# A second z buffer beside the first expert weights, a main load ahead of the last z stores, and another order in the last stage

## The chip, the cores and the metric

The kernel runs on one core of a Trainium2 chip. The metric is device time in microseconds of one execution; lower is better. The kernel before took 805.2 us (median of three runs, 803.65 to 806.26). Its profiled execution took 801.52 us, of which the profile's span covers 799.5 us; times below without another name are counted from the start of that span.

## The reference, cut to what matters

```python
# long convolution over the sequence, by FFT: x (8, 5696, 128), h (5696, 128)
y = irfft(rfft(x, n=2*S, axis=1) * rfft(h, n=2*S, axis=0)[None])[:, :S, :]
# soft mixture of experts on the 45568 rows of y: phi (128, 32), w1 (8, 128, 1024), w2 (8, 1024, 128)
logits = y @ phi
d = softmax(logits over all rows)        # column softmax: it needs every row
slot_in = d.T @ y                        # 32 slots, 4 for each of 8 experts
slot_out[e] = relu(slot_in[e] @ w1[e]) @ w2[e]
c = softmax(logits over the 32 slots)    # row softmax
out = c @ slot_out
```

The output can only be made when the last row of y has been through the column softmax and the experts.

## The kernel before, in words

**The convolution** is a transform in two factors, 90 and 64, written as small matmuls. Batch by batch (h first, then the eight of x) it goes through these stages: `low` and `high` (first transform, L240; result to DRAM in `fl` and `fh`), `loadf` (L274, reads it back in another order as tile `gt`), `forward` (L287 on TensorE, the product with the filter's spectrum on VectorE, L306 and L313), `backward` (L328, evicted by ScalarE into `zst`, L333). What `backward` leaves is stored to DRAM in two parts: the **main** rows in `zm`, which the first eight of a batch's twelve steps fill, and the **rest** rows in `zr`, which the steps 9 to 12 fill. A store isn't issued at once: it is put on a list, and the word `flush` issues the list.

**The pairs.** The second half works on 32 pairs, numbered T, four for each batch; 28 to 31 are those of the last batch. For a pair, on one line each:

- `loadz` (`load_main`, L377) brings 1 MB of main rows into the next buffer of the list `zring`; `loadr` (`load_rest`, L392) brings the rest rows (0.5 MB for the first and second pair of a batch, 1 MB for the third and fourth pair together); `load` does both.
- `product` multiplies them on TensorE (L419 on the main rows, L424 on the rest rows, into the same four banks) and folds the first result on ScalarE and VectorE (L427, L428, L411, L412).
- `sums` adds the rest: L411 and L412 into `op` and `om`, then two additions of `op` on GpSimd (L437) and two of `om` (L437: on GpSimd too, but on VectorE in the last stage).
- `turn` (L447, L449) transposes, `logits` (L456, L461) multiplies by phi, `maximum` (L465, L470, L473) keeps the running column maximum `low` and its step `df`, `exponent` (L487, L491, L496, L500) makes the transposed logits `L` and the column exponentials `dt`, `tokens` (L505, L508) turns `dt` into `d`, `dispatch` (L546, L551) adds to the slot sums `acc`.
- The row softmax: `shift` (maximum L514 on VectorE, subtraction L515 on GpSimd), `exp` (L521 on ScalarE), `rowsum` (L526 to L528 on VectorE), `scale` (L533 on GpSimd), `weights` (L570, transposes the combination weights).

**Where the combination weights go.** The output stage reads them from one tile `cT`. It has room only when the convolution's tiles are gone, so the pairs 0 to 24 write their weights to DRAM (L580, L581). In the last stage `fetch` loads them back in chunks of four pairs (L586, 720 KB, into a ring `cl` of two buffers), and `place2` copies two of the four quarters of a chunk into `cT` on GpSimd (L591, two copies). When the fourth quarter of a chunk is copied, `place` itself calls `fetch_c` for a further chunk. That load needs the buffer of the chunk just copied, so it waits on GpSimd. It is issued on SyncE's queue (SP), as all loads and stores of this stage are, and that queue is in order.

**The order** is written out by hand: a long string of words, each calling one function, fixes the order of issue on every engine at once. Each engine works in order and waits by semaphores.

**Memory.** Tiles come from pools that are opened and closed by hand. `lead` (tiles of the first transform) is closed after `forward` 96, and `w1s`, the first expert weights, takes its place. `front` (filter spectrum, `gt`, `zst`) is closed at the end of the convolution; the pool `last` takes its place. Before the change the list `zring` holds one buffer, `zc`, until then. `zd`, in `last`, is the second, so that no load can go to it before everything that used the memory under it is done.

**The end.** After pair 31: `join` (L598 to L610) brings the four partial maxima together, `inputs` (L784 to L797) makes the experts' inputs `siz`, `hidden` (L807, L812, L814), `flip` (L820, L822) and `second` (L831) are the experts, `outputs` (L840 to L844) makes `so4`. Then the output stage multiplies `cT` by `so4` (L889) and writes 23 MB.

Of the kernel before, what the change touches and what calls it, by code (L numbers as in the profile page):

```python
# [12 lines left out]
F32 = mybir.dt.float32  # L13
# [62 lines left out]
def kernel(  # L76
# [25 lines left out]
    P = 128  # L102
    B, S, D = x.shape
# [6 lines left out]
    CH = 4  # L110
# [245 lines left out]
    zring = [ypool.tile([P, 2, CH, 2, D], F32, name="zc")]  # L356
# [292 lines left out]
    def run(words, batch=0):  # L649
        for word in words.split():  # L650
            name, n = re.fullmatch(r"([a-z]+)(\d*)", word).groups()
            stages[name](*[int(n) + batch * strides.get(name, NQ)] if n else [])
# [26 lines left out]
    for g in range(4):  # L679
# [36 lines left out]
    lead.close()  # L716
    wts = inner.enter_context(tc.tile_pool(name="wts", bufs=1, side="right"))
    w1s = wts.tile([P, E, F], F32, name="w1s")
    run(
# [12 lines left out]
    front.close()  # L732
    rings.append(mid.enter_context(tc.tile_pool(name="ps2", bufs=4, space=PSUM)))
    last = work.enter_context(tc.tile_pool(name="last", bufs=1))
    tail["last"] = last
    zring.insert(0, last.tile([P, 2, CH, 2, D], F32, name="zd"))
    rests.insert(0, last.tile([P, 2, 2, CH, D], F32, name="zy"))
    tail["cT"] = last.tile([P, B, R1, 2 * NJ], F32, name="cT")
    second = inner.enter_context(tc.tile_pool(name="second", bufs=1, side="right"))
# [97 lines left out]
    def join_experts():  # L837
# [8 lines left out]
                  zero=zero_slots, inputs=expert_in, hidden=layer_1, flip=turn_h, second=layer_2,  # L846
                  outputs=join_experts)
    run(
# [11 lines left out]
    assert not (Ls or ys or ds or prods or gs or zs or rest or xs or folded or kept or landed or held)  # L860


# [79 lines left out]
```

## Time and profile before

| what | value |
|---|---|
| median of three runs | 805.2 us (803.65 to 806.26) |
| profiled execution | 801.52 us, span 799.5 us |
| busy share of the span | PE 89%, DVE 79%, ACT 54%, POOL 51% |
| DMA over the span | 353 GB/s |
| last pair's product (L419 on pair 31) starts | 703.15 us |
| `so4` done (VectorE, L844) | 735.35 us |
| output stage | 735.5 us to the end, 398 to 406 GB/s from 750 to 790 us |

PE is TensorE, DVE VectorE, ACT ScalarE, POOL GpSimd, SP SyncE's queue, which here only issues DMAs. In a timeline a row is: start, duration of the group (both us), engine, line, operation, output<-input, shapes, count, and in square brackets how long the engine had been idle before it and what ended the idle time. A row of SP is the issue of a DMA, not its transfer.

### The profile page before, as it was taken

The numbers are of one execution on the slowest core, as the hardware profiler recorded it, in microseconds if no ns is written. First come the engines' busy times: TensorE is split into PE (matmuls) and PEld (weight loads), VectorE is DVE, ScalarE is ACT, GpSimd is POOL, SyncE is SP. The second block draws the span as 40 slices with busy tenths as digits, with TensorE's granted clock in tenths as the row PEclk, the third lists the DMA queues.
The fourth block names the chain that finished last, engine by engine and source line by source line (L and its number), as shares of the span: only waits on it lengthen the run. The fifth ranks groups of instructions, "written<-read, shape, count | busy, mean of one in ns | idle before, by whom it ended". The sixth has DMA issues, their size and how long they took to land.

```text
span 799.5 us, 21830 instructions
## 1 busy us (share of the span) xinstructions
PE 709.9 (89%) x8884; PEld 361.7 (45%) x8884; DVE 629.6 (79%) x895; ACT 428.6 (54%) x868; POOL 410.4 (51%) x368
## 2 busy tenths in 40 slices
PE   6858689869999999999999999999998877888892
PEld 2212233324555444444544455555444444456782
DVE  1039877747999999898999899999998997895542
ACT  2423244426666666666666666666564544674442
POOL 6744242415655666666566666655533453687000
PEclk9989999989999999999999999999999999999765
DMA  8989999999999999999999999999999898873998
GB/s 291 362 301 367 367 380 385 339 360 377 388 345 382 382 396 339 387 388 383 352 396 392 374 365 400 387 359 373 358 333 307 301 376 279 323 280 125 379 401 354
DMA packets 164778, 282.49 MB, mean 353 GB/s; under 512 B 9448, under 2 KB 128872, under 8 KB 158440
## 3 DMA queue, kind: packets, MB, share of 16 engines
q1 hardware_dynamic: 163960, 280.80, 97.1%
q8 instruction: 70, 1.15, 0.5%
q10 hardware_dynamic: 720, 0.31, 0.1%
q14 instruction: 28, 0.23, 0.1%
HBM read 148.54 MB, written 132.53 MB: 352 GB/s over the span
## 4 chain that ended last, share of the span: by engine, by line
PE 62%; DMA 17%; DVE 9%; ACT 5%; issue 2%; SPq 2%; POOL 2%; DVEq 0%; ACTq 0%; POOLq 0%
PE bank L240 21%; PE bt L287 10%; PE bz L328 8%; PE bank L419 6%; DMA out_dram<-o 5%; PE bank L424 4%; PE bank L447 3%; DMA fl<-fst 3%; DMA zx<-zr 3%; PE bank L456 2%; PE bank L546 2%; DVE yf L313 2%; DVE yf L306 2%; DVE bt L306 2%; DMA gt<-fl 2%
## 5 line engine op out<-in xcount | busy, mean ns | idle before, releaser
L216 POOL TENSOR_TENSOR x<-xc 128x512 f32<-128x512 f32 x144 | 179.0, 1275 | 82.9 <-PE bank L240 65.4
L240 PE MATMUL bank<-x,s 128*32 128x512 f32 x1728 | 205.8, 608 | 12.5 <-POOL x L216 7.3
L242 ACT ACTIVATE fst<-bank 128x512 f32<-128x512 f32 x216 | 125.2, 595 | 92.4 <-PE bank L240 76.6
L287 PE MATMUL bt<-gt,wt 64*64 64x256 f32 x1620 | 117.9, 400 | 27.2 <-DMA gt<-fl 10.7
L333 ACT ACTIVATE zst<-bz 128x1024 f32<-128x1024 f32 x96 | 93.0, 969 | 79.4 <-PE bz L328 75.9
L437 POOL TENSOR_TENSOR y<-y,op 128x512 f32<-128x512 f32 x64 | 78.2, 1222 | 107.2 <-DVE op L411 104.7
L306 DVE TENSOR_TENSOR yf<-bt,Hi 128x1024 f32<-128x1024 f32 x96 | 112.5, 1172 | 21.4 <-PE bt L287 21.4
L313 DVE TENSOR_TENSOR yf<-bt,yf 128x512 f32<-128x512 f32 x192 | 119.4, 663 | 3.3
L306 DVE TENSOR_TENSOR bt<-bt,Hr 128x1024 f32<-128x1024 f32 x96 | 113.0, 1177 | 0.0
L240 PEld LDWEIGHTS bank<-x,s 128*32 128x32 f32 x1728 | 53.8, 111 | 127.8 <-issue 88.7
L328 PE MATMUL bz<-yf,vt 64*64 64x256 f32 x1440 | 100.9, 389 | 5.3 <-DVE yf L313 4.8
L287 PEld LDWEIGHTS bt<-gt,wt 64*64 64x64 f32 x1620 | 54.7, 135 | 89.5 <-issue 46.2
L533 POOL TENSOR_TENSOR L<-L,rs 128x512 f32<-128x512 f32 x32 | 34.0, 1063 | 109.2 <-DVE rs L528 90.0
L328 PEld LDWEIGHTS bz<-yf,vt 64*64 64x64 f32 x1440 | 55.1, 136 | 40.9 <-DVE yf L313 12.1
L437 POOL TENSOR_TENSOR y<-y,om 128x512 f32<-128x512 f32 x54 | 64.1, 1188 | 2.1
L427 ACT ACTIVATE y<-bank 128x512 f32<-128x512 f32 x32 | 19.1, 597 | 81.4 <-PE bank L424 81.3
L419 PE MATMUL bank<-zc,im 64*64 64x512 f32 x480 | 60.2, 599 | 0.0
L447 PE MATMUL bank<-ident,y 109*128 109x109 f32 x512 | 58.7, 261 | 1.2 <-ACT yt L449 0.7
L447 PEld LDWEIGHTS bank<-ident,y 109*128 109x128 f32 x512 | 49.7, 141 | 10.1 <-issue 6.8
L449 ACT ACTIVATE yt<-bank 128x360 f32<-128x360 f32 x128 | 52.2, 476 | 1.3 <-PE bank L447 1.2
L306 DVE TENSOR_TENSOR yf<-bt,turn 128x1024 f32<-128x1024 f32 (+1 forms) x12 | 14.0, 1171 | 47.7 <-PE bt L287 47.7
L889 PE MATMUL op<-so,cT 32*128 32x128 f32 x704 | 44.4, 367 | 5.7 <-ACT o L897 5.2
(99 smaller groups left out, 852.9 us busy)
## 6 DMA issues: line engine op xcount, KB each, us to landing
fl<-fst SPq DMA_DIRECT2D x72, 512.0 KB, 7.6
gt<-fl SPq DMA_DIRECT2D x72, 512.0 KB, 6.0
zm<-zst SPq DMA_DIRECT2D x64, 512.0 KB, 9.3
zc<-zm SPq DMA_DIRECT2D x30, 1024.0 KB, 8.8
fh<-fst SPq DMA_DIRECT2D x36, 512.0 KB, 8.3
xc<-in_x_dram SPq DMA_DIRECT2D x32, 512.0 KB, 6.4
out_dram<-o SPq DMA_DIRECT2D x16, 1024.0 KB, 10.1
gt<-fh SPq DMA_DIRECT2D x27, 512.0 KB, 7.5
```

The source lines that it names most:

```text
L216: nc.gpsimd.tensor_tensor(out=y_[:, o, :, :], in0=near, in1=far, op=AL.subtract if o else AL.add)
L240: nc.tensor.matmul(p[i * m:(i + 1) * m, :], s1[:, q + o, cols], columns(c_, o), start=True, stop=True)
L242: nc.scalar.activation(st[:, :, q, :], p[:, :].rearrange("p (n d) -> p n d", d=D), AF.Copy)
L287: nc.tensor.matmul(bt[q * HP:(q + 1) * HP, a, o, :], wt[r, 2 * i + q, :], t_[r, 2 * o + q, :, :].rearrange("p c d -> p (c d)"), start=True ...
L306: nc.vector.tensor_tensor(out=p_, in0=pv, in1=h_, op=AL.mult)
L313: nc.vector.tensor_tensor(out=y_[r, 0:k, c, :], in0=pv[:, :, c, :], in1=y_[r, 0:k, c, :], op=op_)
L328: nc.tensor.matmul(bz[a * HP:(a + 1) * HP, q, o, :], vt[r, i, a, :], y_[r, a * m + o, :, :].rearrange("p c d -> p (c d)"), start=True, sto ...
L333: nc.scalar.activation(zst[:, e_, 0:m, 0:n, :].rearrange("p o q x -> p q o x"), bz[:, 0:n, 0:m, :], AF.Copy)
L419: nc.tensor.matmul(ps[o, c][h_ * HP:(h_ + 1) * HP, :], im[r, c, :], zt[r, h_, :, c, :], start=True, stop=False)
L437: eng.tensor_tensor(out=part_, in0=part(v, 0), in1=o_[:, :, :], op=sign)
L447: nc.tensor.transpose(p[:, i * TR:(i + 1) * TR], ys[T][0:TR, k * CH + i, 0:D], ident[0:TR, 0:TR])
L449: nc.scalar.activation(yt[:, k * CH:(k + 1) * CH, :, :], of_tokens(p), AF.Copy)
```

## The change

The buffer `zd` is allocated right after `w1s`, in the memory that `lead` leaves; from there on the main loads alternate between `zd` and `zc`, pair 25 being the first into `zd`. `loadz28` moves out of the last stage to a place between the `flush` that issues the stores of `backward` 105 and that of `backward` 107. In the last stage the words stand in another order.

```diff
     w1s = wts.tile([P, E, F], F32, name="w1s")
+    zring.insert(0, wts.tile([P, 2, CH, 2, D], F32, name="zd"))
...
-        "maximum25 fetchv5 product26 sums26 backward103 flush loadz27 exponent25 flush "
-        "forward105 backward104 tokens25 shift25 exp25 flush forward106 backward105 dispatch25 "
-        "forward107 backward106 flush rowsum25 flush scale25 turn26 backward107 weights24 "
-        "logits26 flush maximum26 ")
+        "maximum25 fetchv5 product26 sums26 backward103 flush loadz27 exponent25 flush forward105 "
+        "backward104 tokens25 shift25 exp25 flush forward106 backward105 dispatch25 forward107 "
+        "backward106 flush loadz28 rowsum25 flush scale25 turn26 backward107 weights24 logits26 "
+        "flush maximum26 ")
...
-    zring.insert(0, last.tile([P, 2, CH, 2, D], F32, name="zd"))
...
-        "loadz28 loadr28 product27 exponent26 clear shift26 sums27 flush tokens26 spread "
-        "weights25 load29 fetchv6 fetchv7 exp26 fetch fetch dispatch26 flush rowsum26 product28 "
-        "turn27 scale26 sums28 logits27 weights26 maximum27 exponent27 shift27 loadz30 zero "
-        "loadr30 product29 tokens27 exp27 place2 turn28 rowsum27 dispatch27 sums29 loadz31 flush "
-        "scale27 logits28 product30 maximum28 exponent28 place2 turn29 tokens28 shift28 exp28 "
-        "sums30 rowsum28 weights27 logits29 fetchw0 fetchw2 scale28 maximum29 place2 dispatch28 "
-        "exponent29 shift29 product31 turn30 place2 sums31 tokens29 logits30 exp29 weights28 "
-        "place2 rowsum29 fetchw4 dispatch29 scale29 maximum30 turn31 exponent30 logits31 fetchw6 "
-        "flush shift30 weights29 tokens30 exp30 place4 maximum31 rowsum30 exponent31 dispatch30 "
-        "tokens31 scale30 join dispatch31 shift31 weights30 exp31 inputs rowsum31 scale31 place32 "
-        "hidden0 hidden1 flip0 flip1 second0 second1 weights31 outputs ")
+        "loadr28 product27 exponent26 clear shift26 sums27 flush tokens26 spread weights25 fetch "
+        "load29 fetch fetchv6 fetchv7 exp26 dispatch26 flush rowsum26 product28 turn27 scale26 "
+        "place2 sums28 logits27 weights26 maximum27 exponent27 place2 shift27 loadz30 zero "
+        "loadr30 product29 tokens27 exp27 place2 turn28 rowsum27 dispatch27 sums29 loadz31 flush "
+        "scale27 place2 logits28 product30 maximum28 exponent28 turn29 tokens28 shift28 exp28 "
+        "sums30 place2 rowsum28 weights27 logits29 fetchw0 fetchw2 scale28 maximum29 place2 "
+        "dispatch28 exponent29 shift29 product31 turn30 sums31 tokens29 logits30 exp29 weights28 "
+        "rowsum29 fetchw4 dispatch29 scale29 maximum30 turn31 exponent30 logits31 fetchw6 flush "
+        "maximum31 shift30 weights29 tokens30 exponent31 exp30 dispatch30 tokens31 rowsum30 join "
+        "dispatch31 scale30 inputs place2 shift31 exp31 rowsum31 place2 scale31 place32 hidden0 "
+        "weights30 hidden1 flip0 flip1 second0 second1 weights31 outputs ")
```

No instruction is added or taken away; the number of copies into `cT` stays 28.

## The prediction

> **What bounds the kernel now.** I read the chain that ended last, from its end. From 740 us it is the output stores: 398 to 406 GB/s, so this stage starts when `so4` is done and takes what it takes; time won or lost before `so4` (735.35 us) reaches the end one for one. Going back, the last stage hangs on TensorE and VectorE in turn, and its entry is in TensorE's timeline:
>
> ```profile
> 674.12 1.09 PE L546 MATMUL bank<-y,d 128*32 128x129 f32 x32 [0.31 <-ACT d L508]
> 675.77 1.95 PE L419 MATMUL bank<-zd,im 64*64 64x512 f32 x16 [0.56 <-DMA zd<-zm]
> 679.18 1.12 PE L424 MATMUL bank<-zy,ir 26*64 26x512 f32 x16 [1.46 <-DMA zy<-zr]
> ...
> 692.38 1.95 PE L419 MATMUL bank<-zd,im 64*64 64x512 f32 x16
> 694.25 1.11 PE L424 MATMUL bank<-zx,ir 26*64 26x512 f32 x16
> ```
>
> Pair 28 waits for both its loads, pair 30 for neither. Next SP's timeline, since these loads stand in that queue:
>
> ```profile
> 667.68 2.60 SPq L224 DMA_DIRECT2D zr<-zst  x4
> 670.40 0.55 SPq L377 DMA_DIRECT2D zd<-zm  x1
> 672.23 0.32 SPq L392 DMA_DIRECT2D zy<-zr  x1
> ...
> 677.77 0.32 SPq L377 DMA_DIRECT2D zd<-zm  x1
> 679.15 0.32 SPq L392 DMA_DIRECT2D zx<-zr  x1
> 687.02 0.32 SPq L377 DMA_DIRECT2D zc<-zm  x1
> 698.21 0.32 SPq L586 DMA_DIRECT2D cl<-c_t  x1
> ```
>
> The third chunk of weights (698.21) waits for GpSimd's copies of the first (696.48 to 698.18), behind all main loads: harmless. DMA moves 420 to 426 GB/s from 685 to 692.5 us and is all but idle (46 and 58 GB/s) from 695 to 700. Then GpSimd's and VectorE's timelines:
>
> ```profile
> 679.18 1.05 POOL L533 TENSOR_TENSOR L<-L,rs 128x512 f32<-128x512 f32 x1 [0.49 <-DVE rs L528]
> 683.07 2.77 POOL L437 TENSOR_TENSOR y<-y,op 128x512 f32<-128x512 f32 x2 [2.85 <-DVE op L411]
> ...
> 696.48 1.70 POOL L591 COPY cT<-cl 128x352 f32<-128x352 f32 x2
> ```
> ```profile
> 714.39 0.74 DVE L470 SCALAR_TENSOR_TENSOR low<-mx,low 128x1 f32<-128x1 f32 x1
> 715.16 0.97 DVE L473 TENSOR_TENSOR df<-low 128x1 f32<-128x1 f32 x1
> 716.06 0.67 DVE L514 TENSOR_REDUCE rm<-L 128x16 f32<-128x512 f32 x1
> 716.82 0.53 DVE L465 TENSOR_REDUCE mx<-lt 128x1 f32<-128x360 f32 x1
> 717.38 0.49 DVE L470 SCALAR_TENSOR_TENSOR low<-mx,low 128x1 f32<-128x1 f32 x1
> 717.91 0.80 DVE L473 TENSOR_TENSOR df<-low 128x1 f32<-128x1 f32 x1
> ```
>
> VectorE has no gap from 696.05 to 720 us. L470 and L473 take 0.16 us when GpSimd is idle (668.77, 668.96) and 0.49 to 0.97 here, beside its copies and softmax steps.
>
> **Pair 28: 2.05 us earlier.** Main load 28 moves from 670.40 to behind the stores of step 9, about 664.9. DMA moves only 184 to 232 GB/s from 662.5 to 672.5, so 1 MB fits. What it can delay are the stores of step 11 (issued from 667.68, landed 672.02): at most its own 2.5 us (1 MB at 420 GB/s), at least nothing; I take 0.3, as it starts nearly 3 us ahead of them. The rest load, issued at 672.5, then has nothing in front. Idle-queue rows give 2.5 us to landing for 180 KB and 4.2 for 720 KB; in between, 512 KB takes 3.5: landed at 676. TensorE ends L546 at 675.2, runs L419 (1.9) and starts L424 at 677.1, not 679.18. If the stores lose the full 2.5, this gain is gone.
>
> The second buffer also lets load 25 start about 2 us earlier (at 617.92 it waited for pair 24's L419). Pairs 25 to 27 wait for no load, and step 106, which waits 2.11 us for `gt` at 657.66, sits 40 us later: nothing, at most 0.3 us either way.
>
> **Pair 30: a new wait.** The new order copies two quarters before `sums28` and two after it. The second two free the first chunk's buffer, so the fetch of the third chunk is now issued there, on SP **ahead of** loads 30 (main and rest) and 31. It waits for GpSimd: L533 ends 680.23, two copies (1.76) 682.0, L437 (2.77) 684.75, two copies (1.70) **686.45**. Queued behind it: the three loads, issued 677.77 to 687.02 before. By 686.45 the earlier bytes (4.6 MB from 672.5, at the 256 to 423 GB/s of before) are just through. So 720 KB land 4.2 us on, 690.65; main load 30 2.5 later, 693.15; rest load 30 **695.65**. L424 of pair 30 starts there instead of 694.25: **+1.4**. TensorE would have reached it at 693.0 (pair 29's work gains 1.3, as ScalarE waits for `low` of pair 27, now beside copies), so bounds are -1.25 and +2.4 (1 us more of latency).
>
> The Trainium skill, "DMA: Bandwidth & Descriptors", section "Anatomy of one DMA — SWDGE (gpsimd) path", fits 2.0 us plus bytes at 436 GB/s for one DMA on another path. As an estimate by that, the three loads would be in at 694.95 and the sum 0.7 smaller.
>
> **Pair 31: copies away.** VectorE carries the delay to 716. GpSimd's additions for pair 31 no longer start 0.8 late behind a copy, but then they lead VectorE's by 0.7, as in pairs 28 and 29, where VectorE's two took 2.64 and 2.70 instead of 2.29: +0.35. Then L527 falls from 0.44 to 0.17, L470 of pair 30 to about 0.5 (`scale29` still beside it), its L473 and both of pair 31 to 0.16, and L514 (0.67) steps behind them: 0.27 + 0.24 + 0.81 + 0.33 + 0.64 + 0.67 = 2.96. But ScalarE's order (the L496 of pair 30, four `cT` evictions, `d`, L491) takes over as the limit; following it row by row, `dt` of pair 31 ends 5.95 us after VectorE's additions, not 7.30: **-1.35**, with ends 0 and -2.96.
>
> The Trainium skill, "SBUF — State Buffer", section "Who interferes with whom", says a VectorE instruction with two SBUF inputs blocks against a GpSimd one that reads SBUF. It speaks against a larger gain: the copies moved to 680 to 709 block L470 and L473 of pairs 27 and 29 in turn; 0.79 and 0.80 at 704.93 fit.
>
> **`join`.** `exp30` (L521, 717.89 before) now follows `dt` of pair 31 on ScalarE, and `rowsum30` (1.1 us), which needs it, stands ahead of L600 on VectorE. Before, `dt` ended at 719.68 and `acc` of pair 31 began at 722.68, 3.0 later. Now: L521 0.9 after `dt`, three sums 1.15, L600 and L602 0.6, L604 and L546 1.5: 4.2. **+1.2**, between 0 (if L521 slips in early) and 1.6.
>
> **Experts.** `weights30` (L570) moves from the shadow of `acc` between `hidden0` and `hidden1`: **+0.55**; `shift31` moves behind `siz`, so L521 holds ScalarE's first eviction, about hidden by that. The 12 copies left (14 before) end near 738.5, ahead of the batch that needs them.
>
> **Sum:** 1.4 + 0.35 - 1.35 + 1.2 + 0.55 = **+2.15 us**. The profiled execution (801.52) would become 803.7; the median of the runs is 3.7 above it, and 805.2 + 2.15 = **807.4**.
>
> **Rivals.**
> - *The lead reaches the end (faster).* If the fetch is over before pair 30 needs its loads (-1.25 in place of +1.4), and `exp30` costs nothing in `join`: -1.25 + 0.35 - 1.35 + 0 + 0.55 = -1.7; with VectorE rather than ScalarE the limit behind pair 31 (-2.96) -3.3, 801.9. For it: VectorE is packed and copies demonstrably stretch it. Against it: the queue's order is fixed, and so is ScalarE's. Decides: rest load 30 landed before 693.
> - *No stall, but `join` late:* -1.25 + 0.35 - 1.35 + 1.2 + 0.55 = -0.5, 804.7.
> - *The fetch waits longer (slower).* Additions of 3.29 us (710.13) and slower copies put it at 687.5, and loads interleave, as the 6.9 us of pair 28's rest load suggest: L424 at 697.5, +3.25; sum +4.0, 809.2. Decides: fetch after 687.
> - *The load ahead does nothing:* the stores lose all it gains. Pair 30 decides anyway: still about +2.
>
> **The numbers.** Forecast with the last rival (+0.8 to +3.2) 0.52; slower rival 0.20; no stall 0.15; faster rival 0.13. Within 0.3% (2.4 us, about what runs of this kernel can tell apart) lie two thirds of the forecast's 0.52 and most of the no-stall case: 0.46. Slower: 0.20 and a third of the forecast, 0.39. Faster: 0.15 with the edge of the no-stall case. The range reaches into both outer rivals: 802.6 to 810.0.
>
> **What would show it.** Right: L424 of pair 28 at about 677, SP's third fetch at about 686.5 with loads 30 behind it, L424 of pair 30 waiting for DMA to about 695.6, L526 of pair 30 just ahead of L600, L473 of pairs 30 and 31 at 0.16. Wrong: no DMA wait at pair 30, or `acc` of pair 31 within 3 us of `dt`.

## The result, and the profile after

The changed kernel took 813.0 us (median of six runs, 811.2 to 814.1), the kernel before beside it 805.6: a ratio of 1.0106, 95% interval 1.0083 to 1.0128, so about 8.5 us slower by that ratio (the two medians lie 7.5 apart). The forecast was 807.4 with a range up to 810.0: the sign of the forecast was right, the size was not, and the range missed.

The profiled execution took 814.07 us (span 812.3). Of the 12.8 us between the two spans 0.9 lie ahead of pair 27; so I count from the start of pair 27's L419, at 667.45 before and 668.31 after. This pair of traces overstates the difference: the changed kernel's profiled execution is the slowest of its six, while that of the kernel before (801.52) lies below all its six.

TensorE's timeline of the changed kernel (the rows of pairs 28 and 30):

```profile
676.81 2.77 PE L419 MATMUL bank<-zc,im 64*64 64x512 f32 x16
681.75 1.93 PE L424 MATMUL bank<-zy,ir 26*64 26x512 f32 x16 [2.17 <-DMA zy<-zr]
...
699.26 3.48 PE L419 MATMUL bank<-zc,im 64*64 64x512 f32 x16 [3.04 <-DMA zc<-zm]
```

Two things differ from the forecast. Pair 28, which was to reach L424 at 677, reaches it at 681.75, and still waits for its rest load. Pair 30 waits, as forecast, but for the *main* load and 3.04 us, and then the sixteen matmuls of L419 take 3.48 us instead of 1.95. That row, and the 2.77 and 1.93 us of pair 28, lie where TensorE's granted clock (1.00 is full speed) is about half: 0.52 from 675 to 677.5 and from 700 to 702.5, 0.50 from 682.5 to 685. SP's timeline shows what stood in the queue:

```profile
666.25 1.04 SPq L377 DMA_DIRECT2D zc<-zm  x1
...
668.54 3.72 SPq L224 DMA_DIRECT2D zr<-zst  x4
677.38 0.33 SPq L392 DMA_DIRECT2D zy<-zr  x1
...
691.31 0.33 SPq L586 DMA_DIRECT2D cl<-c_t  x1
691.73 0.38 SPq L377 DMA_DIRECT2D zc<-zm  x1
```

The main load of pair 28 stands ahead of the last stores; the rest load, which must wait until they have landed, is issued 8.8 us after the first of them, where it was 4.6 before. The third fetch is issued at 691.31 (forecast 686.45), with pair 30's loads right behind it, as forecast. Why it is so late is in GpSimd's timeline:

```profile
677.24 0.13 POOL L768 MEMSET y<- 128x16 f32 x1 [8.98 <-DMA zr<-zst]
...
683.73 1.74 POOL L591 COPY cT<-cl 128x360 f32<-128x360 f32 x2 [0.63 <-DMA cl<-c_t]
...
689.12 2.15 POOL L591 COPY cT<-cl 128x352 f32<-128x352 f32 x2
```

L768, the memset of a `y` buffer, waits for the last stores from `zst` (before, at 672.38, it waited for ScalarE), and the softmax of pair 26 and the copies that free the fetch's buffer follow in GpSimd's order. The copies also wait 0.63 us for the first chunk itself.

The end, TensorE's timeline:

```profile
726.97 0.27 PE L598 MATMUL bank<-ident,low 128*1 128x128 f32 x1
729.44 0.35 PE L604 MATMUL bank<-one,lr 1*128 1x1 f32 x2 [2.20 <-DVE lr L602]
729.72 1.95 PE L546 MATMUL bank<-y,d 128*32 128x129 f32 x32
...
734.23 3.64 PE L807 MATMUL bank<-w1s,siz 128*32 128x512 f32 x16 [0.28 <-DVE siz L797]
```

and the same stretch in windows of 2.5 us. The columns are the window, its length, busy time and count of PE, PEld, DVE, ACT and POOL, then TensorE's granted clock, DMA share (the mean busy share of the 16 DMA engines) and GB/s. First after:

```profile
727.50:730.00 2.50, 0.56 (x10) 0.55 (x14) 1.64 (x6) 0.66 (x2) 0.97 (x1) 0.94 0.01 3
730.00:732.50 2.50, 2.03 (x34) 1.29 (x26) 1.06 (x2) 0.20 (x1) 1.78 (x3) 0.50 0.00 0
```

then before, first the window with `join`'s wait, then the one with the waits at L784 to L797:

```profile
720.00:722.50 2.50, 1.76 (x39) 1.32 (x37) 0.92 (x5) 0.80 (x2) 2.17 (x3) 1.00 0.80 231
722.50:725.00 2.50, 1.33 (x15) 0.79 (x15) 1.68 (x6) 0.81 (x5) 1.05 (x1) 1.00 0.20 77
```

`join` makes TensorE wait 2.20 us where it waited 0.74. Behind that wait the clock is at half for 10 us (0.50, 0.50, 0.50 and 0.51 in the four windows from 730 to 740, then 1.00): the 32 matmuls of L546 take 1.95 us (1.09 before), the first 16 of L807 take 3.64, in which all 32 were done before. This term stood nowhere in the forecast.

### The profile page after: what moved, and what is told of

The parts are those of the page before. It is cut to its first block, busy times and chain, and to the rows that moved or that the text cites. A ratio compares the mean times of both kernels' runs of the same rounds, so it can differ in the third digit from the quotient of the medians.

```text
span 812.3 us, 21831 instructions
## 1 busy us (share of the span) xinstructions
PE 717.9 (88%) x8884; PEld 365.5 (45%) x8884; DVE 628.0 (77%) x895; ACT 428.7 (53%) x868; POOL 410.6 (51%) x368
## 4 chain that ended last, share of the span: by engine, by line
PE 59%; DMA 18%; DVE 11%; ACT 4%; issue 2%; POOL 2%; SPq 2%; DVEq 0%; ACTq 0%; POOLq 0%
PE bank L240 19%; PE bt L287 9%; PE bz L328 7%; PE bank L419 6%; DMA out_dram<-o 4%; DMA fl<-fst 4%; PE bank L424 4%; PE bank L447 3%; DMA zx<-zr 3%; DMA zr<-zst 2%; DVE yf L306 2%; PE bank L456 2%; PE bank L546 2%; DVE bt L306 2%; DVE yf L313 2%
## 5 line engine op out<-in xcount | busy, mean ns | idle before, releaser
L437 POOL TENSOR_TENSOR y<-y,op 128x512 f32<-128x512 f32 x64 | 77.5, 1212 | 107.4 <-DVE op L411 104.8
L533 POOL TENSOR_TENSOR L<-L,rs 128x512 f32<-128x512 f32 x32 | 34.1, 1065 | 108.1 <-DVE rs L528 89.4
L328 PEld LDWEIGHTS bz<-yf,vt 64*64 64x64 f32 x1440 | 54.6, 134 | 40.0 <-DVE yf L313 12.1
L437 POOL TENSOR_TENSOR y<-y,om 128x512 f32<-128x512 f32 x54 | 64.3, 1191 | 2.1
L419 PE MATMUL bank<-zc,im 64*64 64x512 f32 x448 | 58.8, 622 | 3.0 <-DMA zc<-zm 3.0
L411 DVE TENSOR_TENSOR y<-bank,y 128x512 f32<-128x512 f32 x32 | 22.1, 691 | 37.9 <-ACT y L427 36.4
L521 ACT ACTIVATE L<-L 128x512 f32<-128x512 f32 x32 | 20.2, 631 | 58.1 <-POOL L L515 58.1
```

What stands on the lines that cost most here:

```text
L328: nc.tensor.matmul(bz[a * HP:(a + 1) * HP, q, o, :], vt[r, i, a, :], y_[r, a * m + o, :, :].rearrange("p c d -> p (c d)"), start=True, sto ...
L419: nc.tensor.matmul(ps[o, c][h_ * HP:(h_ + 1) * HP, :], im[r, c, :], zt[r, h_, :, c, :], start=True, stop=False)
L437: eng.tensor_tensor(out=part_, in0=part(v, 0), in1=o_[:, :, :], op=sign)
```

## The experiments

The change has three parts that could lose: the load ahead (`loadz28` before the last stores), the fetch ahead (the third chunk's fetch before pair 30's loads) and the late join (the new order of the end, in which `exp30` comes behind pair 31's exponentials and `rowsum30` right ahead of `join`); and one that could gain (the copies away from pair 31). Every combination of the first three was run, and then kernels in which transposes of the identity fill TensorE's waits, to separate a wait from the clock behind it. (The identity is a constant that lies ready; nobody reads the result.) Theory A: three separate losses. Theory B: nearly all is the load ahead. Theory C: nearly all is the join with its clock. All ratios are to the kernel before, run beside each.

### One part undone at a time

x1_fetch_behind: the third fetch behind the loads of pair 31.

```diff
-                fetch_c()
+                if T_:
+                    fetch_c()
...
-dispatch27 sums29 loadz31 flush
+dispatch27 sums29 loadz31 fetch flush
```

> The changed kernel, with the fetch of the third chunk of weights issued on SP behind main load 31 instead of ahead of main load 30; all copies stay where the change puts them. Theory A (three separate costs: main load 28 ahead of the last stores delays them, the fetch holds up the loads of pair 30, the new end is late at join and TensorE's clock falls there): rest load 28 still lands near 681.7 us, but pair 30's loads now go out as soon as pair 28's buffer is free, so L424 of pair 30 starts near 695 us instead of 702.7; 5 to 7 us faster than the changed kernel, 0 to 3 us slower than before. Theory B (the load ahead of the stores is nearly all of it): at most 2 us faster than the changed kernel. Theory C (join and the clock are nearly all of it): at most 2 us faster.

Measured 809.1 us, ratio 1.0074 (1.0050 to 1.0099): 2.6 us less than the changed kernel by the ratios, where A said 5 to 7, and 6.0 above before, where A allowed 3. B and C (at most 2) lie nearer.

x2_load_behind: pair 28's main load back behind the stores.

```diff
-backward106 flush loadz28 rowsum25
+backward106 flush rowsum25
...
-loadr28 product27
+loadz28 loadr28 product27
```

> The changed kernel, with main load 28 back behind the last z stores, first in the last stage; the rest of the change stays. Theory A: the stores land about 4.3 us earlier (near 672 us on the clock of before), L424 of pair 28 near 679 to 680, the third fetch near 687, L424 of pair 30 near 696; this is what the prediction took for the whole change, so 1 to 4 us slower than before, the upper half if TensorE's clock falls in join. Theory B: within 1 us of before. Theory C: still 6 us or more slower than before.

Measured 812.9, ratio 1.0122 (1.0100 to 1.0144): no gain. This speaks against B, and against the size that A gave the load; it is what C said. In its trace A's steps hold as far as the fetch (L424 of pair 28 comes 11.62 us after the start of pair 27, the fetch 20.42), but L424 of pair 30 comes at 31.39, where A's 696 is 28.5.

x3_join_before: the end in the order of before.

```diff
-maximum31 shift30 weights29 tokens30 exponent31 exp30 dispatch30 tokens31 rowsum30 join
-dispatch31 scale30 inputs place2 shift31 exp31 rowsum31 place2 scale31 place32 hidden0 weights30 hidden1
+shift30 weights29 tokens30 exp30 maximum31 rowsum30 exponent31 dispatch30 tokens31 scale30 join
+dispatch31 shift31 weights30 exp31 inputs rowsum31 scale31 place32 hidden0 hidden1
```

> The changed kernel, with the words from pair 31's maximum to the end of the last stage in the order of before (exp30 ahead of pair 31's exponent, weights30 ahead of the experts, copies all at the end). Theory A: the gap in TensorE's work in join shrinks from 2.2 to below 1 us and its clock stays at 1.0 there, so 3 to 5 us faster than the changed kernel, 2.5 to 5 us slower than before; L424 of pair 30 stays near 702. Theory B: within 1 us of the changed kernel. Theory C: within 1 us of before.

Measured 810.0, ratio 1.0077 (1.0056 to 1.0097). The clock stays at 1.00 from `join` on. It is still 6.2 us slower than before, more than A's 2.5 to 5, so C is not enough.

x4_load_ahead_alone: before, with only `zd` allocated early and `loadz28` ahead.

> The kernel before, with only the second z buffer beside the first expert weights and main load 28 ahead of the last z stores; the words of the last stage as before. Theory A: the last stores land about 4 us later than before, L424 of pair 28 starts 1.5 to 2.5 us later, nothing is held up by a fetch; 1.5 to 3.5 us slower than before. Theory B: 6 us or more slower than before. Theory C: within 1 us of before.

Measured 805.4, ratio 1.0025 (1.0006 to 1.0045), so 2.0 us slower: within A, and B is out.

### The other combinations

x5_all_three (all three undone; what is left are the moved copies, the place of `zd`, and the fetches of the first two chunks, one of which the change also puts ahead of `load29`):

> The changed kernel with all three things undone: the main load of pair 28 behind the z stores, the third fetch behind the main load of pair 31, the end in the order of before. What is left of the change is the place of the second z buffer and the weight copies of L591, which stand in earlier pairs and no longer in the last. Theory A (three separate costs, nothing else): the copies' absence from pair 31 gained 1.7 us between L424 of pair 30 and L505 of pair 31, so this kernel comes out 0 to 2 us faster than before, 802 to 804 where before gives 804. Rival (the copies cost more in the pairs that they were moved to, which is why putting the load behind gained nothing): 2 to 5 us slower than before.

Measured 804.4, ratio 0.9981 (0.9960 to 1.0002).

x8_fetch_ahead_alone (the edits of x2 and x3) and x9_load_ahead_rest_undone (those of x1 and x3):

> The changed kernel with the load of pair 28 behind the z stores and the end in the order of before, but the third fetch still ahead of the loads of pair 30. Beside the kernel without all three, this one prices the fetch alone. Theory A: the third fetch is issued some 18 us after the start of the last z stores, and pair 30's main load behind it; TensorE waits for that load, pair 30 begins 3 to 5 us later than before, and 1.7 us come back in pair 31: 1.5 to 3.5 us slower than before. Rival (the wait is hidden when the stores are not delayed): within 1 us of the kernel with all three undone.

> The changed kernel with the third fetch behind the loads of pair 31 and the end in the order of before, but pair 28's main load still ahead of the last z stores. Beside the kernel without all three, this one prices the load ahead alone. Theory A: the last z stores land some 4 us later, the memset L768 and the softmax of pair 26 with them; what reaches TensorE is 1 to 3 us by pair 30, and 1.7 us come back in pair 31: 0 to 2 us slower than before. Rival (the load ahead is nearly all of the loss): 5 us or more slower than before.

Measured 809.8, ratio 1.0051 (1.0032 to 1.0070), and 805.1, ratio 0.9994 (0.9974 to 1.0014). Between x5 and x8 lies only the fetch: 5.6 us, more than A said. x9 is within A and far from its rival.

x10_join_alone (the edits of x1 and x2):

> The changed kernel with the load of pair 28 behind the z stores and the third fetch behind the loads, but its own late join: beside the kernel with all three undone (ratio 0.998 to before) it prices the late join alone. Theory A (join is late by 1.5 us, one transpose group stands among the expert layers, and the clock falls to 0.5 over the layers): 5 to 7 us slower than the kernel with all three undone, a ratio of 1.0045 to 1.0065 to before. Rival (the join costs its own latency only, and what the changed kernel lost beyond that was the fetch): 1.5 to 2.5 us slower, a ratio of about 1.0005.

Measured 810.5, ratio 1.0076 (1.0051 to 1.0101): 7.6 us above x5, a little more than A, and far from its rival.

The eight kernels in one table; each is one step from its neighbours:

| load ahead | join late | fetch behind | fetch ahead | the fetch costs |
|---|---|---|---|---|
| no | no | 0.9981 (x5) | 1.0051 (x8) | 0.0070 |
| yes | no | 0.9994 (x9) | 1.0077 (x3) | 0.0083 |
| no | yes | 1.0076 (x10) | 1.0122 (x2) | 0.0046 |
| yes | yes | 1.0074 (x1) | 1.0106 (after) | 0.0032 |

Mean over four steps each, times 805 us: the fetch ahead costs 4.7 us (0.0058), the late join 5.5 us (0.0069: 0.0095, 0.0080, 0.0071, 0.0029), the load ahead 0.4 us (0.0005: steps from -0.0016 to +0.0026). A single step is known only to about 0.003, a mean of four to about half of that, 1.2 us. x4 has the load ahead in the words of before and puts it at 2.0 us (0.5 to 3.6), so its price lies between nothing and about 2 us. Fetch and join cost less together than one by one; with steps this uncertain that is no finding.

How the fetch costs so much is in TensorE's timeline of x8:

```profile
699.65 3.69 PE L419 MATMUL bank<-zc,im 64*64 64x512 f32 x16 [3.90 <-DMA zc<-zm]
703.27 1.84 PE L424 MATMUL bank<-zx,ir 26*64 26x512 f32 x16
```

beside that of x5, where the row waits for nothing:

```profile
694.49 1.95 PE L419 MATMUL bank<-zc,im 64*64 64x512 f32 x16
```

and, in x8's GpSimd and SP, with the chain that sets the fetch when no store is late:

```profile
685.18 1.72 POOL L591 COPY cT<-cl 128x360 f32<-128x360 f32 x2 [1.51 <-DMA cl<-c_t]
686.85 3.28 POOL L437 TENSOR_TENSOR y<-y,op 128x512 f32<-128x512 f32 x2
```
```profile
691.81 0.33 SPq L586 DMA_DIRECT2D cl<-c_t  x1
```

Counted from pair 27 (670.90 here), the fetch is issued at 20.9 us; the forecast had 19.0 (686.45 less 667.45). In x5 the fetch goes out at 20.4, no earlier, but behind the loads, and TensorE doesn't wait: the place in the queue is what costs. GpSimd's 1.51 us of waiting for the first chunk and 0.5 more in L437 are that difference. So even without the late stores the fetch came later than forecast.

### The waits filled

The added transposes write a bank that the next matmul overwrites, and nothing else differs. y1 has twelve in `join` of the changed kernel:

```diff
+        for i in range(12):
+            nc.tensor.transpose(p[:, (1 + i % 3) * P:(2 + i % 3) * P], ident[:, :], ident[:, :])
         nc.tensor.matmul(p[:, 0:1], lr[:, :, :].rearrange("p k s -> p (k s)"), one[:, :],
```

> The changed kernel with twelve more transposes of the identity on TensorE in the wait of join (between L598 and L604), into a bank that L604 writes afterwards; nothing else differs. They stand in a wait of 2.20 us and take about 2.0 us at the full clock (four such transposes are 0.66 us in L505's row). Theory A (TensorE's clock falls because it stood idle at join, and the expert layers pay for it): the granted clock stays at 1.0 or near it over the layers, L807 to L831 takes 5.5 to 6.5 us as in before instead of 8.9, and the time falls by 2.5 to 4 us. Rival (the clock falls for another reason, such as the wait for pair 30's loads): the clock is again 0.5 over the layers, and the time is the changed kernel's within 0.5 us, or longer.

Measured 812.6, ratio 1.0085 (1.0057 to 1.0114). Neither theory's size: they took 1.47 us, left 0.81 us of the wait, and the clock fell some 4 us later, for about 3.5 us instead of 10; L604 to L831 took 11.5 us instead of 13.7. The waits of 0.5 and 0.9 us at L784 and L793 were still there. So y3 fills all:

> The changed kernel with transposes of the identity on TensorE in all its waits behind the two new late points: 24 ahead of pair 30's first matmul, 17 in join, 3 ahead of L784 and 6 ahead of L793, each group into a bank that the next matmul overwrites. Nothing else differs. Twelve of them took 1.47 us in join, so the groups fill about 2.9, 2.1, 0.4 and 0.7 us. Theory A (an idle TensorE loses its clock, and the work behind pays double): the clock stays at 1.0 from pair 30 to the end of the layers, L419 of pair 30 takes 1.95 us and L807 to L831 5.5 to 6.5 us, and the time falls by 4 to 6 us, to a ratio of about 1.004. Rival (the clock falls for a reason that these transposes don't touch, or the transposes themselves come too late): the time falls by less than 2 us, as with the join alone filled.

Measured 811.0, ratio 1.0078 (1.0049 to 1.0107). A window of y3 between `join` and the layers, those on both sides of it (from 730 to 740) have 1.00 too:

```profile
732.50:735.00 2.50, 2.18 (x17) 1.20 (x21) 1.42 (x5) 0.00 (x0) 0.56 (x2) 1.00 0.00 0
```

TensorE is busy for 2.18 us where it was 1.33 in the same window of the changed kernel, the clock stays at 1.00, and L604 to L831 takes 9.9 us (13.7 in the changed kernel, 9.2 before). That half of A is shown. The time fell by 2.3 us by the ratios, the part of the trace behind pair 27 by 4.3; with an interval of about 2 us to each side of either ratio that is not settled by this kernel. Two cleaner ones were run, each with one loss.

y4 is x8 with 24 transposes ahead of pair 30's first matmul:

> The kernel with the third fetch ahead of pair 30's loads as its only loss, with 24 transposes of the identity on TensorE ahead of pair 30's first matmul, where it waits 3.90 us for the main load. Theory A (of the 5.4 us that the fetch costs, 3.8 are the wait and 1.7 the half clock behind it): the wait stays, L419 of pair 30 takes 1.95 us instead of 3.69, and the time falls by 1 to 2 us, to a ratio of about 1.003. Rival (the later loads set the time, so that a faster L419 only waits for the rest load): L424 starts no earlier, and the time stays within 0.5 us.

Measured 808.0, ratio 1.0051 (1.0032 to 1.0070), that of x8, as the rival said. TensorE's timeline of y4 (its lines lie 3 higher; the transposes ran from 693.89 for 2.84 us):

```profile
697.23 1.95 PE L422 MATMUL bank<-zc,im 64*64 64x512 f32 x16 [0.50 <-DMA zc<-zm]
699.72 1.12 PE L427 MATMUL bank<-zx,ir 26*64 26x512 f32 x16 [0.54 <-DMA zx<-zr]
```

The main product runs at the full clock, and then TensorE waits for the rest load. The trace is not quite the rival's: L424 comes 30.98 us after the start of pair 27, in x8 32.37, and at L831 0.85 us of these 1.4 are left. The two ratios are equal, give or take 2.2 us. So at pair 30 it is the queue that costs; what the clock adds is not seen in the times, and about 1 us of it can't be ruled out.

z1 is x10 with the join's waits filled:

> The kernel whose one loss is the late join (ratio 1.0076 to before), with the transposes of the identity in join's waits: 17 ahead of L604, 3 ahead of L784, 6 ahead of L793. Theory A (of what the late join costs, about 1.5 us is its latency, 0.5 the transposes of pair 30 among the layers and the rest the half clock): the clock stays at 1.0, from L604 to the first matmul of L831 it takes 9.9 us as with all waits filled, not 12.1, and the time falls by 2 to 4 us. Rival (the order of the end costs it, on VectorE and ScalarE, and TensorE's clock has nothing to do with it): from L604 to L831 it takes 11.5 us or more at the full clock, and the time stays within 1 us.

Measured 803.8, ratio 1.0004 (0.9982 to 1.0027), down from 1.0076: 5.8 us gained, more than A said. TensorE's timeline of x10:

```profile
728.37 0.35 PE L604 MATMUL bank<-one,lr 1*128 1x1 f32 x2 [2.21 <-DVE lr L602]
728.65 1.73 PE L546 MATMUL bank<-y,d 128*32 128x129 f32 x32
...
740.51 3.70 PE L832 MATMUL bank<-w2s,zc 128*32 128x128 f32 x128
```

and of z1:

```profile
719.33 2.02 PE L605 MATMUL bank<-ident 128*128 128x128 f32 x17
721.61 0.38 PE L606 MATMUL bank<-one,lr 1*128 1x1 f32 x2 [0.26 <-DVE lr L602]
721.92 1.09 PE L546 MATMUL bank<-y,d 128*32 128x129 f32 x32
...
731.52 3.70 PE L838 MATMUL bank<-w2s,zc 128*32 128x128 f32 x128
```

From the matmul of `join` to the first of the second layer: 12.1 us in x10, 9.9 in z1. The wait for VectorE is as long in both; only TensorE's idleness is gone. So the late join costs about 2 us by itself (z1 above x5: 0.0023, 1.9 us; by the traces 1.5 up to L604 and 0.7 from there to L831), and the half clock the rest: 2.2 us by this trace, 5.8 by the times, give or take 2.7.

The other traces bear this out. From L604 to L831 it takes 12.1, 12.1, 12.6 and 13.7 us in the four kernels with the late join and nothing filled (x2, x10, x1 and the changed kernel), each at half clock behind the wait; 9.9 with all waits filled (y3, z1); and 9.2 in all nine kernels with the order of before, whose clock stays at 1.00 there. That puts the half clock at 2.2 to 3.8 us and the whole late join at 4.4 to 6.0, around the 5.5 of the table.

### The gain that is left

x12 is before with the copies moved, the first two fetches where the change has them and the third behind (x5 without the early `zd`):

> The kernel before with only the weight copies of L591 in earlier pairs, and the third fetch behind the main load of pair 31, where nothing waits behind it; the second z buffer stands where it stood before. It differs from the kernel with all three undone by that buffer alone. Theory A (the copies' absence from pair 31 is the one gain, the buffer's place brings nothing): 0.5 to 2 us faster than before, a ratio of 0.9975 to 0.9995, the same as with the buffer moved. Rival (the buffer's place brings the gain): the time of before, and the kernel with all three undone 1 us or more ahead of it.

Measured 802.6, ratio 0.9985 (0.9967 to 1.0002). x5 and x12 agree: the moved copies, with the first two fetches, are worth about 1.4 us, the place of `zd` nothing that these runs can tell. Each interval touches 1, so this is likely, not certain; that the gain lies in pair 31 shows in the traces alone (below). These two are the best versions found, and the early load is not needed for them.

z2 is x12 with 16 transposes ahead of step 106's matmuls, at the other wait with a low clock behind it:

> The kernel before with only the weight copies in earlier pairs (ratio 0.9985 to before), with 16 transposes of the identity ahead of the matmuls of step 106, which wait 1.82 us for their load; the clock stands at 0.65 for the 5 us behind that wait in the kernel before. Theory A (idleness takes the clock wherever it falls): the clock stays at 1.0 there, and the pairs behind begin 0.5 to 1.5 us earlier; the time falls by as much if TensorE sets the end there, to a ratio of 0.997 to 0.998. Rival (VectorE and the DMA set the time in that stretch): the clock stays at 1.0 and the time does not change, within 0.3 us.

Measured 806.9, ratio 1.0021 (1.0003 to 1.0038): slower, which neither expected. TensorE's timeline of z2 (lines 3 higher):

```profile
658.39 1.97 PE L285 MATMUL bt<-ident 128*128 128x128 f32 x16 [1.68 <-ACT zst L336]
```

The transposes needed step 106's bank, which ScalarE frees only at the end of the wait; so they filled nothing and stood in front of the real work, 4.24 us from the start of L505's row to the first matmul instead of 2.48 in x12. The clock did stay at 1.00 there, but the experiment says nothing on what that is worth.

## Why the prediction was wrong, point by point

Two terms of the sum failed. The wait of pair 30 stood at +1.4 us and measured 4.7: the queue was right, the time of the fetch was not. `join` and the experts stood together at +1.75 and measured 5.5: the sum put the clock behind `join`'s longer wait at nothing, without a reason. The error on pair 28 is a third, but the sum counts from pair 30 and did not contain it. The sign came out right because the queue and the late `join` were rightly seen.

- **Pair 28: 2.05 earlier.** Wrong in sign. The failed step is "at most its own 2.5 us ... I take 0.3". In the changed kernel the last stores were 4.3 us late, by the issue of the rest load; pair 28's L424 comes 13.44 us after the start of pair 27, not 11.73. In the seven kernels with the load ahead the rest load is issued 6.2 to 8.8 us after the first of the last stores, in the others 4.5 to 4.9; L424 follows at 10.90 to 13.44 us, in the others at 11.3 to 11.9. I read room from "only 184 to 232 GB/s". The same windows had a DMA share of 0.61 to 0.93; after, one is full at 252 GB/s. A window before:

```profile
667.50:670.00 2.50, 2.50 (x35) 0.69 (x32) 0.85 (x3) 0.53 (x2) 0.00 (x0) 1.00 0.61 184
```

  and after:

```profile
667.50:670.00 2.50, 2.50 (x26) 0.67 (x24) 0.85 (x3) 1.17 (x4) 0.76 (x1) 1.00 1.00 252
675.00:677.50 2.50, 2.50 (x36) 1.72 (x40) 2.06 (x4) 0.48 (x4) 0.26 (x2) 0.52 0.09 26
```

  The GB/s overstated the room: by the share, about a fifth of the 10 us was free, some 2 us, where 1 MB at 420 GB/s needs 2.5. Why the stores lost up to 4.3 us, more than the load's own 2.5, no run shows. The 1 MB moved into the stores' time, and the time that it left stands nearly empty (26 GB/s) while SP waits for the stores. That this costs little in the end (0.4 us in the table, 2.0 in x4) is near to what the rival "the load ahead does nothing" said. The traces behind pair 27 have it between 0.6 us better and 4.1 worse at L831; its size stays open.
- **Pair 30: a new wait, +1.4.** The mechanism was right: the fetch waits for GpSimd, and the loads stand behind it. The size was not: 4.7 us. In x8 the fetch came 1.9 us late because I let GpSimd's copies follow L533 at once; they wait for the first chunk, and I had not asked when that lands. Pair 30's main product started 7.8 us after the fetch (699.65 less 691.81), where the forecast had main load 30 in 6.7 after it. The condition of my rival "the fetch waits longer" (fetch after 687) holds in x8, where the fetch is at 688.4 on the clock of before. That its 809.2 is near x8's 809.8 is luck: it contains the `join` and the experts, which x8 doesn't change. Without them the rival had +2.25 us, and x8 is 4.1 above before.
- **Pair 31: -1.35 and +0.35.** About right. From L424 of pair 30 to L505 of pair 31: 25.48 us before, 24.77 in x5, 24.31 in x12, 23.80 after: -0.7 to -1.7 for a forecast of -1.0. (In the changed kernel the new order of the end is in this figure too.) VectorE's rows are as forecast, L473 at 0.16 in pairs 30 and 31:

```profile
722.92 0.16 DVE L473 TENSOR_TENSOR df<-low 128x1 f32<-128x1 f32 x1
...
725.06 0.16 DVE L473 TENSOR_TENSOR df<-low 128x1 f32<-128x1 f32 x1
```

- **`join` +1.2, experts +0.55.** Right as far as they went: L505 to L604 takes 2.97 us instead of 1.51 (+1.46), with L526 of pair 30 just ahead of L600, and with the clock kept the way from L604 to L831 takes 9.9 instead of 9.2 (+0.7).
- **What the sum lacked** is the clock behind a longer wait. The profile before showed such falls, the nearest 0.64 and 0.67 at 657.5 to 662.5 us behind the wait of step 106, and no step of mine used them. In the changed kernel L604 to L831 takes 13.7 us, 3.8 more than with the clock kept. The Trainium skill, "TensorE: Matmul & The Clock Gate", section "Part 1: The HAM clock gate", gives half rate after an idle window of about 3.4 us; the trace here has half rate after a wait of 2.20 us (0.56 us busy in 2.5), so a limit on the single gap would have passed this change, and the measurement decides.

Measured in the same terms: 4.7 + 5.5 + 0.4 - 1.4 = 9.2 us, beside 8.5 measured for the whole.

## What to carry to other kernels

When a wait on the path grows, price the clock behind it too: look up what the granted clock did behind waits of about that length in the profile of before, and take the next stage at full and at half clock as the two ends of the range, since one trace doesn't tell which it will be (below). For room for a transfer look at the DMA share as well as at the GB/s. A load that waits for a buffer holds up everything behind it in its queue, so follow the buffer's whole chain, including the landing of the data that is in it, before putting such a load ahead of others.

## What the runs showed of the hardware that I had not expected

- A wait of 2.2 us among small matmuls was followed by 10 us at a granted clock of 0.50, although TensorE was busy for the last 5 of them; filling the wait, and two of 0.5 and 0.9 us behind it, kept 1.00. Filling only most of it moved the fall some 4 us on and shortened it.
- The half clock comes in pieces of one length. A window of 2.5 us at 0.50 was at half throughout, one at 0.64 for 1.8 us. Added up so, it lasts 3.4 us behind step 106 in before (0.64 and 0.67), 3.4 in y1 (0.85, 0.50, 0.96), 6.8 behind `join` in x10 (0.79, 0.50, 0.50, 0.85) and 10.2 in the changed kernel: one, two and three times 3.4.
- The length of a wait alone doesn't decide. The wait of 1.75 or 1.76 us ahead of the first L505 behind pair 27's product (672.78 in before) is there in all 16 profiled executions. In seven of them the clock fell to a half behind it (in the changed kernel from 675 us on), in nine, before among them, it stayed at 1.00.
- At 252 GB/s the DMA's busy share was 1.00 while the last stores and a load of 1 MB ran together.
- Pair 27 starts between 667.17 and 673.83 us in the 16 profiled executions, though the programs differ little ahead of it. The end of one trace can't carry a difference of 0.5%; stretches behind a common point can, and the medians of the runs.
